# Pooled attention with a mixture-of-depths layer: one value load per batch, natural key order, no stores from GpSimd, a new order

## The chip, the core and the metric

The kernel runs on one core of a Trainium2 chip. The metric is the device time of one execution in microseconds (us). A profile is one execution recorded by the hardware: it gives the busy time of the engines (PE is the matmul engine, DVE the vector engine, ACT the scalar engine, POOL is GpSimd, SP the sync engine, which here only issues DMAs), the waits, and the traffic of the 16 DMA engines.

## The reference

Inputs are q, k and v of 8 batches, 8 heads, 576 tokens and 64 elements in float32, a gate vector and two weight matrices.

1. Keys and values are averaged over groups of 8 tokens, so each head has 72 pooled keys and values. Scores are q times pooled keys, scaled; softmax over the 72; output is the weighted sum of pooled values. The heads side by side make x of 576 x 512 per batch.
2. Each token of x gets a score by the gate vector. The 128 highest tokens of a batch (`capacity`) go through relu(x W1) W2, with W1 of 512 x 1024 and W2 of 1024 x 512; the result is multiplied by the sigmoid of the score and added to the token. All other tokens of x are returned as they are.

## The kernel before, in words

`direct_path` (line 253) does all of it; a general path behind a flag is not entered with these inputs. Step functions are named here by what they do, with the short names that the order tables use; `b` is the batch, `h` a half of the tokens, `c` one of five chunks of the tokens.

- **Loads.** `load_kq` (L472) and `load_v` (L485) issue them, all on SP's queue. Keys of a batch come in one load of 1.15 MB into the one buffer KR (`k`); queries in two of 0.64 and 0.51 MB (`q{b}{h}`); values of two heads side by side: 64 of the 72 pooled groups of each head on 128 partitions in four loads of 256 KB (`v{b}a` to `d`), the 8 groups left over of each head in four loads of 64 KB to 32 partitions each. Two of these four are copies of the other two, for two blocks of 32 partitions. In the main part group 9 of each nine is the leftover. Weights `w1{g}`, `w2{g}` are four loads of 1 MB.
- **Pooling.** Batch 0 is pooled on PE (`kP`, `vP`). Other batches on DVE or POOL (`kp`, `va`, `vb`), in place. `kh` transposes pooled keys in 32 x 32 blocks, `kt` (L546) adds the last pair and splits main keys from leftovers, `kl` (L551) spreads the leftover keys over a block of zeros. `vg`, `vt` give the values' part of the gate score, `vl` (L640) spreads the leftover values.
- **Attention.** `qt` transposes queries (DVE). `s` and `sl` are the scores of a half (PE, four PSUM banks that only one half can hold at a time), `x` and `xl` their exponentials (ACT), `a{b}{c}` weighted sums of a chunk (PE), `z`, `r`, `n` divide by the sum (ACT, DVE), `o{b}{c}` (L703) stores the chunk to the output in HBM: 256 KB, or 128 KB for chunk 4.
- **Selection.** `sc`, `sp`, `ke`, `c`, `oh`, `pk`, `tk` rank the tokens and find the 128 indices; `ix` (L768) on POOL gathers these rows from the output in HBM, for which all five stores of the batch must have landed.
- **Dense layers.** `tu` transposes the gathered rows, `u{b}{g}{f}` are the 8 column blocks of W1 (PE, L800; 8 matmuls each), `re` the relu, `d{b}{f}` the 8 row blocks of W2 (PE, L814), `y` the residual, `pt` (L822) on POOL scatters the rows to the output.

What sets the order: each step is registered with `add` in a `Plan` (L106); every engine runs its steps strictly in the order of the table ORDER (L48, a list of step numbers); HOMES picks the PSUM banks, and TURNS picks the engine where a step allows several (the costs that stand with the steps are used only when there is no table). A DMA of SP's or ACT's queue takes one of eight completion counters in turn, and the program makes it wait until the DMA eight places earlier in the table, of either queue, has landed. An engine that issues such a DMA waits there with all that is behind it. DMAs of POOL have counters of their own.

Of the kernel before, what the change touches and what calls it, by code (L numbers as in the profile page):

```python
# [11 lines left out]
OP = mybir.AluOpType  # L12
# [4 lines left out]
def kernel(  # L17
# [60 lines left out]
"""  # L78
HOMES = """
# [3 lines left out]
"""  # L83
TURNS = """
# [15 lines left out]
"""  # L100
TABLE = [[int(x) for x in t.split()] for t in (ORDER, HOMES, TURNS)]
ON_PE = (0,)
AGO = 500


class Plan:  # L106


    SWITCH = 0.2
# [143 lines left out]
def direct_path(ctx, tc, q, k, v, moe_w_gate, moe_w1, moe_w2, moe_capacity, out, flag):  # L253
# [6 lines left out]
    nc = tc.nc  # L260

    B, H, S, D = q.shape
    POOLW = 8
    SP = S // POOLW
    G = 16
# [150 lines left out]
    def opening():  # L416
# [12 lines left out]
        def line():  # L429
# [3 lines left out]
            for x in (*SS, *RZ):  # L433
                nc.gpsimd.memset(x, 0.0)
# [816 lines left out]
```

## Time and profile before

| what | value |
|---|---|
| runs shown | 263.66, 265.09, 265.61 us, median 265.09 us |
| profiled execution | 264.04 us, of which the span of instructions is 262.3 us |
| mean granted PE clock | 0.955 of full |
| busy in the span | PE 225.8 us (86%), DVE 150.5 us (57%), ACT 88.1 us (34%), POOL 99.9 us (38%) |
| DMA | 47.88 MB, of which HBM reads 35.78 MB |
| chain that ended last | DMA 38%, PE 37%, issue 7%, DVE 5%, POOL 5% of the span |

The time of the profiled execution has 1.74 us around the span. PE's busy share is not its efficiency: matmuls overlap, so the time that a stretch of work takes is read from the starts of the rows, not from their lengths. The 40 slices of the page show two stages: the DMA engines are at 0.97 or more of full use until about 80 us, and at 0.6 to 1.0 until 150 us; from 156 us on PE is busy nearly without a break until 252 us, and a tail of some 10 us follows (last residual, scatter and flag).

### The profile page before, as it was taken

How to read it: one execution, taken by the hardware profiler on the slowest of the kernel's cores; microseconds unless marked ns; L12 is line 12 of the kernel's file. 1: busy time of each engine (PE TensorE's matmuls, PEld its weight loads, DVE VectorE, ACT ScalarE, POOL GpSimd, SP SyncE). 2: the span in 40 equal slices, each digit the busy share in tenths (PEclk: the TensorE clock that was granted, in tenths of full speed). 3: DMA queues.
4: the chain of work that ended last, by engine and by line, in shares of the span. 5: the costliest groups of instructions: out<-in, count | busy, mean ns of one | idle time of the engine just before them, and what ended most of it. 6: DMA issues, size and time to landing. Idle time of an engine off the chain costs nothing.

```text
span 262.3 us, 7373 instructions
## 1 busy us (share of the span) xinstructions
PE 225.8 (86%) x3074; PEld 158.2 (60%) x3074; DVE 150.5 (57%) x346; ACT 88.1 (34%) x302; POOL 99.9 (38%) x154
## 2 busy tenths in 40 slices
PE   5599698974896899999898789999799989999960
PEld 5486546543485545974776356866399757759430
DVE  5059978654675567686887893848366136100310
ACT  1013566765124715811167232467141000110100
POOL 5014569925753266026073870112333520120120
PEclk9999979999799599999999979999999999999995
DMA  5999999999997768499968510013116520110120
GB/s 163 312 269 288 315 304 360 316 300 306 313 387 286 246 208 275 142 259 323 296 197 308 188 44 2 2 42 103 43 41 202 159 83 2 34 46 2 40 77 15
DMA packets 18413, 47.88 MB, mean 183 GB/s; under 512 B 2964, under 2 KB 2964, under 8 KB 17476
## 3 DMA queue, kind: packets, MB, share of 16 engines
q1 hardware_dynamic: 13776, 37.75, 45.1%
q0 software_dynamic: 2896, 6.76, 8.3%
q10 hardware_dynamic: 1700, 2.82, 3.3%
q8 instruction: 26, 0.43, 0.7%
q14 instruction: 15, 0.12, 0.1%
HBM read 35.78 MB, written 11.53 MB: 180 GB/s over the span
## 4 chain that ended last, share of the span: by engine, by line
DMA 38%; PE 37%; issue 7%; DVE 5%; POOL 5%; SPq 2%; ACT 2%; ACTq 0%; POOLq 0%; DVEq 0%
DMA qr<-in_q_dram 10%; PE pJ L800 9%; DMA vr<-in_v_dram 9%; DMA out_dram<-y,ix 6%; DMA w<-in_moe_w_dram 5%; PE pG L814 5%; PE pJ L814 4%; PE pG L800 4%; DMA out_dram<-xs 4%; DMA xr<-out_dram,ix 4%; PE pG L581 3%; PE pA L814 3%; SPq L400 2%; PE pA L658 2%; PE pG L590 2%
## 5 line engine op out<-in xcount | busy, mean ns | idle before, releaser
L800 PEld LDWEIGHTS pJ<-xg,w 128*128 128x128 f32 x352 | 41.6, 194 | 5.9 <-issue 5.1
L800 PE MATMUL pJ<-xg,w 128*128 128x128 f32 x352 | 43.6, 280 | 0.0
L744 DVE SCALAR_TENSOR_TENSOR cmp<-sr,sc,lat 128x576 bf16<-128x576 f32 (+1 forms) x40 | 36.6, 916 | 1.3 <-ACT sr L412 0.7
L814 PE MATMUL pJ<-w,ht 128*128 128x512 f32 x64 | 31.9, 636 | 0.0
L581 PE MATMUL pG<-qt,kt 32*64 32x256 f32 (+1 forms) x512 | 22.9, 447 | 3.5 <-issue 2.4
L563 DVE STREAM_TRANSPOSE qt<-qr 128x1280 f32<-128x1280 f32 (+1 forms) x16 | 21.8, 1365 | 5.9 <-DMA qr<-in_q_dram 5.8
L595 ACT ACTIVATE em<-pG 128x1280 f32<-128x1280 f32 (+1 forms) x16 | 18.2, 1138 | 11.7 <-PE pG L590 11.7
L623 POOL TENSOR_TENSOR vr<-vr 128x512 f32<-128x512 f32 (+1 forms) x11 | 16.7, 1541 | 7.4 <-DMA vr<-in_v_dram 3.8
L684 DVE RECIPROCAL rz<-za 128x8 f32<-128x8 f32 (+1 forms) x40 | 7.4, 190 | 20.9 <-ACT za L676 17.9
L814 PEld LDWEIGHTS pJ<-w,ht 128*128 128x128 f32 x64 | 11.9, 201 | 11.5 <-issue 11.1
L769 POOL TENSOR_SCALAR ix<-tk 128x1 int32<-128x1 f32 x8 | 2.3, 284 | 41.4 <-DVE gv L778 19.0
L581 PEld LDWEIGHTS pG<-qt,kt 32*64 32x64 f32 x512 | 10.5, 138 | 11.6 <-issue 7.7
L658 PEld LDWEIGHTS pG<-vs,em 64*64 64x64 f32 x528 | 13.0, 141 | 5.4 <-ACT em L595 3.0
L658 PE MATMUL pA<-vs,em 64*64 64x66 f32 x480 | 12.9, 224 | 3.8 <-issue 3.1
L814 PE MATMUL pA<-w,ht 128*128 128x512 f32 x32 | 15.8, 596 | 0.0
L823 POOL DMA_INDIRECT out_dram<-y,ix x8 | 8.7, 1088 | 18.4 <-DVE y L819 14.6
L658 PE MATMUL pG<-vs,em 64*64 64x66 f32 x528 | 13.9, 230 | 2.1 <-ACT em L595 2.1
L658 PEld LDWEIGHTS pA<-vs,em 64*64 64x64 f32 x480 | 10.8, 135 | 7.9 <-issue 5.4
L800 PEld LDWEIGHTS pG<-xg,w 128*128 128x128 f32 x128 | 14.8, 192 | 1.0 <-issue 1.0
L800 PE MATMUL pG<-xg,w 128*128 128x128 f32 x128 | 15.2, 276 | 0.0
L814 PE MATMUL pG<-w,ht 128*128 128x512 f32 x32 | 14.4, 592 | 0.0
L693 ACT ACTIVATE xs<-pA,rz 128x64 f32<-128x64 f32 (+1 forms) x64 | 14.0, 348 | 0.0
(173 smaller groups left out, 387.7 us busy)
## 6 DMA issues: line engine op xcount, KB each, us to landing
vr<-in_v_dram SPq DMA_DIRECT2D x32, 256.0 KB
kr<-in_k_dram SPq DMA_DIRECT2D x7, 1152.0 KB
qr<-in_q_dram SPq DMA_DIRECT2D x8, 640.0 KB
qr<-in_q_dram SPq DMA_DIRECT2D x8, 512.0 KB
w<-in_moe_w_dram SPq DMA_DIRECT2D x4, 1024.0 KB
out_dram<-xs SPq DMA_DIRECT2D x15, 256.0 KB
out_dram<-xs ACTq DMA_DIRECT2D x9, 256.0 KB
vr<-in_v_dram SPq DMA_DIRECT2D x32, 64.0 KB
```

The source lines that it names most:

```text
L400: i = engine(e).dma_start(out=dst, in_=src)
L563: nc.vector.transpose(out=QT[b % 2][h].rearrange("p j t c -> p t j c"), in_=QR[b % 2][h].rearrange("p t (j e) -> p t j e", j=2))
L581: note(nc.tensor.matmul(pG[64 * s : 64 * s + 64, r, 0:n], KT[i][rows, j, s, 0:NK], tokens(j, s, rows, 0, hi - lo), start=(j == 0), stop=(j ...
L595: note(nc.scalar.activation(EM[h][i], pG[:, :, 0:n], AF.Exp, scale=exp_scale))
L623: engine(e).tensor_tensor(out=x[:, a:z, 0:4], in0=x[:, a:z, 0:4], in1=x[:, a:z, 4:8], op=OP.add)
L658: note(nc.tensor.matmul(acc[64 * z : 64 * z + 64, s, E * m : E * m + E], EM[h][i][64 * s : 64 * s + 64, m, m0 + 64 * z : m0 + 64 * z + 64] ...
L684: nc.vector.reciprocal(RZ[i][rows, c], ZA[rows, b, c])
L693: note(nc.scalar.activation(to[:, s, m], o[:, s, m, 0:D], AF.Copy, scale=rz[:, NP * s + m : NP * s + m + 1]))
L744: nc.vector.scalar_tensor_tensor(cmp[0:n], SR[0:n], SC[i][0:n, c : c + 1], LAT[0:n, LAST - OFF[c] : LAST - OFF[c] + S], op0=OP.subtract, o ...
L800: note(nc.tensor.matmul(single(ju)[:, cap * f : cap * f + cap], w1[g][:, d, 128 * f : 128 * f + 128], XG[i][:, d, :], start=(d == 0), stop ...
L814: note(nc.tensor.matmul(single(jd)[0:cap, :], HT[i][f // 4][:, f % 4, :], w2[f // 4][:, f % 4, :], start=(f == 0), stop=(f == FB - 1)))
L823: j = nc.gpsimd.indirect_dma_start(out=out_rows, out_offset=bass.IndirectOffsetOnAxis(ap=IX[x][:, :1], axis=0), in_=Y[i], in_offset=None)
```

## The change

- Values: the main part of a batch is one load of 1 MB. Its partitions hold groups 8 to 71 of the even head and groups 0 to 63 of the odd head, which lie next to each other in HBM. The leftovers (groups 0 to 7 of the even, 64 to 71 of the odd head) come in two loads of 64 KB rather than four; the second copy of 32 partitions is made on the core, after pooling, by a new step `vd` of two small copies on ACT (5 batches) or DVE (3).
- Keys stay in natural order: `kt` adds all 288 pairs in one instruction, scores read shifted columns of it, `kl` is one instruction instead of two.
- Queries: one buffer and one load of 1.15 MB per batch (batch 0 keeps two).
- Stores `o` can no longer go to POOL. Before, 17 were on SP, 12 on ACT and 11 on POOL; after, 21 on SP and 19 on ACT.
- Four memsets on POOL at the start, 32 x 512 each.
- New ORDER, HOMES and TURNS. DMAs of SP and ACT: 123 before, 88 after.

```diff
-    QR = [[sb(f"qr{i}{h}", [128, hi - lo, D]) for h, (lo, hi) in enumerate(HALF)] for i in range(2)]
+    QR = sb("qr", [128, TG, D], n=2)
...
-        alts = (("SP", cost), ("ACT", cost), ("POOL", 0.75)) if free else (("SP", cost),)
+        alts = (("SP", cost), ("ACT", cost)) if free else (("SP", cost),)
...
+            for x in VR:
+                for z in (32, 96):
+                    nc.gpsimd.memset(x[z : z + 32, NP], 0.0)
...
+            dma(QR[b % 2], src, 128 * 256 * TG, p + 2, (), [("QR", b % 2, 0), ("QR", b % 2, 1)], name=f"q{b}")
...
-        for m in range(NP):
-            dma(VR[i][:, m], bass.AP(tensor=t, offset=o + 2 * m * head, ap=[[(NL + 1) * run, G], [run, NL], [1, run]]),
-                128 * 2048, p + 0.01 * m, [("VR", i, m // 2)], [("VRq", i, m)], name=f"v{b}{'abcd'[m]}", cost=0.6)
+        dma(VR[i][:, 0:NP], bass.AP(tensor=t, offset=o + NL * run, ap=[[run, 128], [2 * head, NP], [1, run]]),
+            128 * NP * 2048, p, [("VR", i, 0), ("VR", i, 1)], [("VRq", i, 0)], rate=390e3, name=f"v{b}", cost=0.6)
         for s in range(2):
-            src = bass.AP(tensor=t, offset=o + s * head + NL * run, ap=[[(NL + 1) * run, NL], [2 * head, NP], [1, run]])
-            for u in range(2):
...
+            dma(VR[i][64 * s : 64 * s + 32, NP], bass.AP(tensor=t, offset=o + s * (SP + NK) * run, ap=[[run, NL], [2 * head, NP], [1, run]]),
+                32 * 2048, p + 0.3 + 0.1 * s, [("VR", i, 1)], [("VRq", i, 1 + s)], rate=110e3, name=f"v{b}{s}", cost=0.65)
-    VQ = ((0, 1), range(2, 8))
+    VQ = ((0,), (0, 1, 2))
...
+            engine(e).tensor_tensor(out=KT[i][:, :, 0 : 2 * SP], in0=x[:, :, :, 0], in1=x[:, :, :, 1], op=OP.add)
...
+        def again(e):
+            for s in range(2):
+                of = VS[i][64 * s : 64 * s + 32, NP]
+                to = VS[i][64 * s + 32 : 64 * s + 64, NP]
...
+        both((("DVE", 0.35), ("ACT", 0.42)), False, again, [("VS", i)], [("VS2", i)], p, name=f"vd{b}")
```

The tables name steps by number. Decoded, these are the parts that the prediction speaks of (in the new table `v3` is the main load of batch 3, `v30` and `v31` its leftovers; in the old one a leftover has three digits):

```
SP before:  q01 v000 k01 k00 v1a v0b v0a v0c v0d v010 v001 v011 q00 v1b k1 v101 v100 v1d v111 v1c v110 q11 v2d k2
            v200 v2a v2c v201 v211 v210 v2b q10 q20 q21 v311 k3 o02 v3c v301 q40 v310 q31 q41 o04 v3a v300 q30 v3b
            w21 v3d w11 v4c w10 o13 v4b k4 w20 q51 o11 v410 v400 v411 v4a v4d v401 k5 ...
SP after:   k01 q01 k00 v0 v10 v01 v00 q00 k1 v11 v1 q1 k2 v2 q2 k3 v20 v21 v31 q3 v3 v30 w20 w10 o03 o04 k4 o11
            w11 o12 v41 o10 v4 o24 q4 v40 o23 w21 k5 v51 v50 v5 q5 ...
PE before:  ... pk0 sp10 a22 a20 a24 a21 tu0 sp11 s31 sl31 a23 u010 u011 s30 sl30 u012 u013 u000 u001 u002 u003
            sp21 a33 a32 a34 pk1 d00 ...
PE after:   ... pk0 sl31 a24 a20 s30 sl30 tu0 a32 a33 a30 u010 u011 u012 u013 u000 u001 u002 u003 pk1 a31 a34
            s41 sl41 d00 d01 d02 d03 tu1 s40 sl40 a44 ...
ACT after:  ... xl30 o14 ge0 xg0 o13 z30 z32 oh1 n32 re00 o21 z31 o32 z34 o31 o20 x41 xl41 n34 ...
POOL after: ... va30 va31 vb3 vg3 ix0 kp41 vl3 pc1 va40 va41 gp0 kt4 kl4 vb4 vg4 ix1 ...
Eight places before (new table): o14 after k4, o13 after v41, o32 after w21, o31 after v51, o20 after v50, o40 after k6
```

## Rows read from the trace of the kernel before

**Rows 1.** Stretches: us, busy of PE, PEld, DVE, ACT, POOL (instructions), PE clock, DMA share, GB/s.

```profile
60.00:70.00 10.00, 5.10 (x100) 3.00 (x100) 5.81 (x13) 3.44 (x19) 5.67 (x8) 0.90 1.04 312
80.00:90.00 10.00, 6.65 (x116) 4.70 (x114) 4.26 (x9) 6.19 (x20) 2.40 (x2) 0.75 0.64 237
156.00:252.00 96.00, 93.16 (x1004) 66.37 (x1003) 40.00 (x119) 22.68 (x65) 20.15 (x38) 1.00 0.19 57
```

**Rows 2.** The chain that ended last: start us, us, what.

```profile
56.93 14.20 DMA w<-in_moe_w_dram
...
102.22 1.05 PE pG L581 x32
103.27 0.57 PE pG L590 x16
103.84 0.63 PE pA L658 x32
104.47 0.45 PE pA L662 x8
...
245.38 6.88 PE pG L814 x16
```

**Rows 3.** PE's timeline at the first dense layer: start us, us, instructions, idle before and releaser.

```profile
66.80 0.63 PE L791 MATMUL pA<-ident,xr 128*128 128x128 f32 x4 [2.62 <-DVE qt L563]
72.26 2.05 PE L800 MATMUL pJ<-xg,w 128*128 128x128 f32 x16
86.35 1.16 PE L658 MATMUL pG<-vs,em 64*64 64x66 f32 x32 [1.88 <-ACT em L595]
```

**Rows 4.** ACT's timeline in the same stretch.

```profile
71.16 0.57 ACTq L400 DMA_DIRECT2D out_dram<-xs  x1
73.31 0.18 ACT L677 COPY ss<-pA 128x8 f32<-128x8 f32 x1
81.59 0.62 ACTq L400 DMA_DIRECT2D out_dram<-xs  x1
82.31 0.60 ACT L807 ACTIVATE ht<-pJ 128x512 f32<-128x512 f32 x1 [8.82 <-DVE qt L563]
85.29 1.00 ACT L595 ACTIVATE em<-pG 128x1024 f32<-128x1024 f32 x1
```

**Rows 5.** Stretches again, for the rate of the DMA engines (last column).

```profile
0.00:70.00 70.00, 53.20 (x951) 37.81 (x955) 45.57 (x93) 29.50 (x111) 36.12 (x62) 0.96 0.97 295
10.00:16.00 6.00, 6.00 (x22) 4.65 (x22) 1.48 (x9) 0.40 (x1) 0.00 (x0) 1.00 1.05 253
22.00:28.00 6.00, 5.41 (x141) 4.18 (x137) 5.64 (x10) 2.98 (x6) 1.51 (x1) 1.00 1.03 248
32.00:36.00 4.00, 3.10 (x56) 1.49 (x64) 3.22 (x8) 1.59 (x12) 3.16 (x3) 0.73 0.99 244
76.00:80.00 4.00, 4.00 (x37) 4.00 (x38) 3.93 (x9) 0.00 (x0) 0.00 (x0) 1.00 1.03 406
```

**Rows 6.** Groups by line and form: count, busy us, mean ns of one, idle before.

```profile
L400 POOL DMA_DIRECT2D out_dram<-xs x11 | 7.5, 684 | 6.9 <-DMA out_dram<-y,ix 5.3 <-ACT xs L693 1.5
L641 POOL TENSOR_TENSOR vl<-vs,inside 128x528 f32<-128x528 f32 x6 | 6.9, 1146 | 10.0 <-DVE rz L684 6.7 <-DVE vs L637 2.3 <-DMA kr<-in_k_dram 1.0
L532 POOL TENSOR_TENSOR kr<-kr 128x512 f32<-128x512 f32 x1 | 1.7, 1743 | 0.0
L533 POOL TENSOR_TENSOR ks<-kr 128x256 f32<-128x256 f32 x1 | 0.9, 861 | 0.1
L412 ACT COPY vs<-pG 128x128 f32<-128x128 f32 x1 | 0.3, 266 | 1.4 <-PE pG L613 1.4
L434 POOL MEMSET rz<- 128x40 f32 x2 | 0.2, 170 | 0.0
```

**Rows 7.** Who waited for whom: us in total, times, longest.

```profile
POOL kx L553 <- DVE kh L541: 24.2, 3, 13.1
```

**Rows 8.** Issues of chunk stores on ACT: ns min/median/max, first and last start.

```profile
L400 ACTq DMA_DIRECT2D out_dram<-xs x12: 564/614/1189, 39.1 to 202.9; - x12
```

More of the change, by code (lines that the diff above doesn't have):

```diff
@@ L305, in direct_path @@
     KH = sb("kh", [128, 2, 2 * G, R])
-    KT = sb("kt", [128, 2, 2, NK], n=2)
-    KX = sb("kx", [128, 2, 2, NL], n=2)
+    KT = sb("kt", [128, 2, 2 * (SP + NK)], n=2)
     KL = sb("kl", [128, 2, 2, NL, NP], n=2)
@@ L434, in line @@
                 nc.gpsimd.memset(x, 0.0)
+            for x in VR:
+                for z in (32, 96):
+                    nc.gpsimd.memset(x[z : z + 32, NP], 0.0)
             nc.gpsimd.memset(RK, -1.0)
-        add("POOL", 2.2, line, (), ["first", "slots"] + [(x, i, c) for x in ("SS", "RZ") for i in range(2) for c in range(NC)]
-            + [("RK", b, c) for b in range(B) for c in range(NC)], -89, name="line")
+        add("POOL", 3.4, line, (), ["first", "slots"] + [(x, i, c) for x in ("SS", "RZ") for i in range(2) for c in range(NC)]
+            + [("RK", b, c) for b in range(B) for c in range(NC)] + [("VR", i, 1) for i in range(2)], -89, name="line")
         def grid():
@@ L481, in load_kq @@
         src = q[b].rearrange("h (g t) d -> (h g) t d", g=G)
-        for h, (a, z) in enumerate(HALF):
-            dma(QR[b % 2][h], src[:, a:z], 128 * 256 * (z - a), p + 2 + 0.1 * h, (), [("QR", b % 2, h)], name=f"q{b}{h}")
+        if b == 0:
+            for h, (a, z) in enumerate(HALF):
+                dma(QR[0][:, a:z], src[:, a:z], 128 * 256 * (z - a), p + 2 + 0.1 * h, (), [("QR", 0, h)], rate=345e3, name=f"q{b}{h}")
+        else:
+            dma(QR[b % 2], src, 128 * 256 * TG, p + 2, (), [("QR", b % 2, 0), ("QR", b % 2, 1)], name=f"q{b}")
     def load_v(b):
@@ L487, in load_v @@
         o, t, run, head = v.offset + b * H * S * D, v.tensor, POOLW * D, S * D
-        for m in range(NP):
-            dma(VR[i][:, m], bass.AP(tensor=t, offset=o + 2 * m * head, ap=[[(NL + 1) * run, G], [run, NL], [1, run]]),
-                128 * 2048, p + 0.01 * m, [("VR", i, m // 2)], [("VRq", i, m)], name=f"v{b}{'abcd'[m]}", cost=0.6)
+        dma(VR[i][:, 0:NP], bass.AP(tensor=t, offset=o + NL * run, ap=[[run, 128], [2 * head, NP], [1, run]]),
+            128 * NP * 2048, p, [("VR", i, 0), ("VR", i, 1)], [("VRq", i, 0)], rate=390e3, name=f"v{b}", cost=0.6)
         for s in range(2):
-            src = bass.AP(tensor=t, offset=o + s * head + NL * run, ap=[[(NL + 1) * run, NL], [2 * head, NP], [1, run]])
-            for u in range(2):
-                x = 64 * s + 32 * u
-                dma(VR[i][x : x + 32, NP], src, 32 * 2048, p + 0.3 + 0.1 * s, [("VR", i, 1)], [("VRq", i, 4 + 2 * s + u)],
-                    rate=104e3, name=f"v{b}{s}{u}", cost=0.65)
-    VQ = ((0, 1), range(2, 8))
+            dma(VR[i][64 * s : 64 * s + 32, NP], bass.AP(tensor=t, offset=o + s * (SP + NK) * run, ap=[[run, NL], [2 * head, NP], [1, run]]),
+                32 * 2048, p + 0.3 + 0.1 * s, [("VR", i, 1)], [("VRq", i, 1 + s)], rate=110e3, name=f"v{b}{s}", cost=0.65)
+    VQ = ((0,), (0, 1, 2))
     def load_gate():
@@ L542, in k_trans @@
         add("DVE", 1.25, one, [("KS", 0), ("KS", 1)], ["KH"], 100 * b - 60, name=f"kh{b}")
-        x = KH.rearrange("p j c r -> p (j c r)").rearrange("p (a n two) -> p a n two", n=NL + 1, two=2)
+        x = KH.rearrange("p j c r -> p j (c r)").rearrange("p j (n two) -> p j n two", two=2)
         def two(e):
-            engine(e).tensor_tensor(out=KT[i].rearrange("p j s (a n) -> p (j s a) n", n=NL), in0=x[:, :, 0:NL, 0], in1=x[:, :, 0:NL, 1],
-                                    op=OP.add)
-        both((("DVE", 0.45), ("POOL", 0.63)), True, two, ["KH"], [("KT", i)], 100 * b - 60, name=f"kt{b}")
+            engine(e).tensor_tensor(out=KT[i][:, :, 0 : 2 * SP], in0=x[:, :, :, 0], in1=x[:, :, :, 1], op=OP.add)
+        both((("DVE", 0.45), ("POOL", 0.67)), True, two, ["KH"], [("KT", i)], 100 * b - 60, name=f"kt{b}")
         def three(e):
-            e = engine(e)
-            e.tensor_tensor(out=KX[i].rearrange("p j s a -> p (j s a)"), in0=x[:, :, NL, 0], in1=x[:, :, NL, 1], op=OP.add)
-            e.tensor_tensor(out=KL[i].rearrange("p j s n m -> p (j s) n m"),
-                            in0=KX[i].rearrange("p j s (n one) -> p (j s) n one", one=1).to_broadcast([128, 4, NL, NP]),
-                            in1=inrow.rearrange("p (a b m) -> p a b m", a=1, b=1).to_broadcast([128, 4, NL, NP]), op=OP.mult)
-        both((("DVE", 0.45), ("POOL", 0.6)), True, three, ["KH", "ident"], [("KL", i)], 100 * b - 60, name=f"kl{b}")
+            left = KT[i].rearrange("p j (s n one) -> p (j s) n one", s=2, one=1)[:, :, 0:NL]
+            engine(e).tensor_tensor(out=KL[i].rearrange("p j s n m -> p (j s) n m"), in0=left.to_broadcast([128, 4, NL, NP]),
+                                    in1=inrow.rearrange("p (a b m) -> p a b m", a=1, b=1).to_broadcast([128, 4, NL, NP]), op=OP.mult)
+        both((("DVE", 0.33), ("POOL", 0.42)), True, three, [("KT", i), "ident"], [("KL", i)], 100 * b - 60, name=f"kl{b}")
     def q_trans(b, h):
@@ L563, in go @@
             nc.vector.transpose(out=QT[b % 2][h].rearrange("p j t c -> p t j c"),
-                                in_=QR[b % 2][h].rearrange("p t (j e) -> p t j e", j=2))
+                                in_=QR[b % 2][:, lo:hi].rearrange("p t (j e) -> p t j e", j=2))
         add("DVE", 0.19 + 0.0653 * (hi - lo), go, [("QR", b % 2, h)], [("QT", b % 2, h)], 100 * b - 55 + 10 * h, name=f"qt{b}{h}")
@@ L580, in go @@
                     for s in range(2):
-                        note(nc.tensor.matmul(pG[64 * s : 64 * s + 64, r, 0:n], KT[i][rows, j, s, 0:NK],
+                        note(nc.tensor.matmul(pG[64 * s : 64 * s + 64, r, 0:n], KT[i][rows, j, (SP - NL) * s + NL : (SP - NL) * s + SP],
                                          tokens(j, s, rows, 0, hi - lo), start=(j == 0), stop=(j == 1)))
@@ L638, in pool_v @@
         add("DVE", 0.48, total, [("VS", i)], [("VR", i, 0), ("VR", i, 1), ("VS2", i)], p, name=f"vt{b}")
+        def again(e):
+            for s in range(2):
+                of = VS[i][64 * s : 64 * s + 32, NP]
+                to = VS[i][64 * s + 32 : 64 * s + 64, NP]
+                if e == "ACT":
+                    nc.scalar.copy(out=to, in_=of)
+                else:
+                    nc.vector.tensor_copy(to, of)
+        both((("DVE", 0.35), ("ACT", 0.42)), False, again, [("VS", i)], [("VS2", i)], p, name=f"vd{b}")
         def spread(e):
```

91 rows, old and new, of tables (HOMES, ORDER, TURNS) are left out of this document.

## The prediction, made before the changed kernel was run

> **What bounds the kernel now.** I read the stretches first. The time falls in two. From 156 us to the end of the matmuls at 252 us PE is busy for 93.2 of 96 us at the full clock and the DMA engines at a fifth [rows 1]; the chain ends there in PE's second dense layer [rows 2]. So the end is PE's, and a step counts only if it lets PE start its work sooner or takes a hole out of it. The holes lie before: in 60 to 70 us PE is busy for 5.1 of 10 us, in 80 to 90 us for 6.65, there at a mean clock of 0.75 [rows 1]. Then I read the chain for what ends these two.
>
> The first hole ends with weights. PE turns the gathered rows of batch 0 at 66.80 us, but the first column block of W1 starts at 72.26 us [rows 3], after the load `w11`, issued at 56.93 us, has landed 14.2 us later [rows 2]. 1 MB alone needs 2.6 us at 406 GB/s, so the load stood in a queue: the DMA engines are full from the start (0.97 over 70 us) but move 295 GB/s on average [rows 5]. The rate is lost where leftovers land: 253, 248 and 244 GB/s in three stretches in which three, four and four of these small loads come, against 406 GB/s in a stretch without [rows 5].
>
> The second hole is ACT's. Its store `o14` goes out at 71.16 us, just as `w11` lands, which stands eight places earlier in the table; it finished a copy at 73.5 us and then stood at the issue of the next store, `o12`, until 81.59 us; the relu and the exponential behind it came at 82.31 and 85.29 us, and PE's next chunk at 86.35 us [rows 3, 4]. The hole costs 3.35 us of idle time [rows 1] and, from 86.35 to 90 us at the half clock (1.2 of 2.4 GHz, the mean of 0.75 says so), some 1.8 us more: 5.2 us.
>
> **The parts.** The sum is made against the profiled execution, 264.0 us, which lies 1.05 us under the median of the runs.
>
> Leftover loads, 32 to 16. What one costs beyond its bytes: 10 to 16 us moved 1.52 MB, which at 406 GB/s takes 3.74 us, so 2.26 us are lost on three, 0.75 us each; the same in the other two stretches gives 0.58 and 0.40 us [rows 5]. I take their mean over eleven, 0.56 us; ends 0.40 and 0.75. Ahead of `w11` in SP's table stand 16 of them before and 8 after: 4.5 us less (3.2 to 6.0). But the new order puts more large loads and the stores ahead: summed by the table, 19.5 MB with `w11` before, 20.0 after. The rate without leftovers is 20.65 MB in 70 - 2 (before the first load) - 16 x 0.56 = 59 us, 0.35 MB/us [rows 5], so 0.5 MB is 1.4 us. `w11` lands at 71.16 - 4.5 + 1.4 = 68.1 us, and `k4`, 1.3 MB ahead of it, at 64.4 us.
>
> Four value loads of 256 KB in one of 1 MB. By the table the stretch with 406 GB/s holds loads of 256 KB to 1.15 MB and shows no size that is slow, so by bytes and rate this is worth nothing; 64 issues on SP become 24, and SP is no bound. The Trainium skill ("DMA: Bandwidth & Descriptors", Rules for kernel authors) asks for at least 1 MiB per DMA for the full rate and calls transfers under 64 KB mostly overhead. If loads of 256 KB paid what leftovers do, the twelve fewer in four batches, at 0.56 us, would take 6.7 us more off the way to `w11`; no run here shows such a price, and the sum is made without it.
>
> The new order at the first dense layer. PE no longer waits for `w11` alone: `s30`, `a30`, `a32` and `a33` now come before `u010`, all of batch 3. Prices: a half's scores 1.05 + 0.57 = 1.62 us, a chunk 0.63 + 0.45 = 1.08 us [rows 2], so 4.9 us of work moves into the hole of 60 to 70 us. But these chunks need `vl3`, and on POOL that is now behind `kp41`, which needs `k4`: 64.4 + 1.74 + 0.86 for `kp41`, + 1.15 for `vl3` [rows 6], + 3.24 for three chunks gives 71.4 us, with 0.2 us for the hand-overs 71.6 us for `u010`, against 72.26. So the dense stage starts 0.7 us sooner and with 4.9 us less left to do: -5.6 us (ends 0, where the batch-3 work is late by as much as it is worth, and -8.9 us, where `w11` alone decides).
>
> Later leftovers, eight less, 4.5 us of DMA time after 72 us. There the DMA engines are no longer full (0.64 in 80 to 90 us [rows 1]), so most of it is beside PE's work: I take -1.5 us, ends 0 and -4.5.
>
> Stores off POOL. Eleven issues of 0.68 us and 6.9 us of waiting leave POOL [rows 6]; four go to SP and seven to ACT at 0.61 us [rows 8], 4.3 us more on an engine that is busy for a third. Beside other work they cost nothing; if ACT is late for PE at each, 4.3 us. With `vd` I take +0.5 us. `vd` is two small copies per batch, nearest a copy of 128 x 128 at 0.27 us [rows 6], so 0.5 us per batch between `vt` and `vl`; POOL and PE have other steps in between, and without these all eight would cost 4.3 us.
>
> Queries in one load: the half that is scored first waits for all 1.15 MB, 1.9 us longer at 0.35 MB/us for its 0.64 MB partner. Where the old order loaded the halves apart the second came much later, so I take 0, ends -2 and +2. The memsets on POOL (nearest 0.17 us [rows 6]; for 512 columns at most a few times that) lie in a wait of 13.1 us [rows 7]; one `kt` of 288 pairs and one instruction less in `kl`: nothing. Both are covered unless POOL becomes late; then about 1 us once.
>
> Sum: -5.6 - 1.5 + 0.5 = -6.6 us: 257.4 us for a profiled execution, 258.5 us as a median. The ends of the terms, not all at once, span 251 to 266.
>
> **Rivals.** *More than that:* the second hole closes too, because `w20` and `w10` now land before `w11`, so that fewer large loads are still under way when ACT comes to its stores. Against it: the new table still has ACT issuing four stores there. It gives 5.2 us more, 253, and with the full wire gain down to 247. Chance 0.16.
>
> *Nothing gained:* the bound of the first stage is not the wire but the chain pooling, transposes, ranking on DVE and POOL (DVE busy 45.6 of 70 us [rows 5], with waits for loads among the rest); then `u010` comes as much later as it has more done before it, and the time is 262.5 to 267. For it: `vl3` behind `kp41` as above. Chance 0.18.
>
> *Slower:* ACT stands behind stores. Seven more are on ACT, and each waits for the DMA eight places earlier, which is now `k4` for `o14`, `v41` for `o13`, `w21` for `o32`, leftovers of batch 5 for `o31` and `o20`, `k6` for `o40`: loads of 1 MB or small ones queued behind such. The price of one such stand that reaches PE is 5.2 us, as above. The profile already has one of 8 us [rows 4]. It decides from two more stands on that reach PE: 258.5 + 2 x 5.2 = 269 us. For it: `x41`, which `a44` needs, stands behind four stores in ACT's table. Against it: PE has the whole first layer of batch 0 and four `d` in front of `a44`. Chance 0.18.
>
> That the change does not do what it says (a leftover's price is one of the batch, not of the load, so that two cost what four did) leaves 1 MB less to read, 3 us over the run; it is in the second rival.
>
> **The numbers.** My forecast, 253 to 262, has 0.48. About 1% is what a measurement of this kernel can tell from no change, so the bounds are 262.4 and 267.7 us. Faster: 0.48 + 0.16 = 0.64; same 0.18; slower 0.18. The range leaves 0.05 below and 0.13 above: 248 to 267.
>
> **What would show it.** Right: `w11` lands near 68 us, the rate over the first 70 us is 310 GB/s or more, `u010` starts at 71 to 72 us with four steps of batch 3 behind it, and 156 to the end is full as before, some 6 us earlier. Wrong: a first 70 us no faster on the wire (then a leftover's price is elsewhere); ACT idle for over 5 us in front of an issue of a store and PE idle behind it (the slower rival); PE waiting for `vl3` or for a transposed query with the loads long landed (nothing gained).

## The result and the profile after

The changed kernel takes 252.67 us in the median (249.60 to 256.79), beside 264.53 us for the kernel before; the ratio is 0.9475 with a 95% interval of 0.9377 to 0.9574. Two later comparisons give 0.9504 (0.9340 to 0.9669) and 0.9507 (0.9400 to 0.9614). So it is faster by 5%, some 13 us, where 6.6 us were forecast. Runs of one kernel spread by some 3%, and the ratios here and below are made from those within 1.5% of each kernel's fastest.

| profiled execution | before | after |
|---|---|---|
| time, span | 264.04, 262.3 us | 249.60, 247.8 us |
| busy PE, DVE, ACT, POOL | 225.8, 150.5, 88.1, 99.9 us | 220.0, 146.1, 83.4, 106.9 us |
| DMA | 47.88 MB | 46.82 MB |
| last load issued | 143.81 us | 112.35 us |
| chain: PE, DMA | 37%, 38% | 60%, 16% |

The stretches of the kernel after that answer to [rows 1, 5], with the end of the run at 240 where it was at 252 (columns as there):

```profile
0.00:70.00 70.00, 53.14 (x1043) 36.94 (x1043) 54.27 (x103) 31.59 (x111) 39.03 (x63) 0.95 0.91 322
10.00:16.00 6.00, 5.23 (x33) 4.33 (x32) 4.48 (x14) 0.27 (x1) 0.99 (x1) 1.00 1.01 350
32.00:36.00 4.00, 2.69 (x79) 1.50 (x80) 2.81 (x6) 2.74 (x10) 3.16 (x4) 1.00 0.96 339
60.00:70.00 10.00, 8.03 (x181) 5.42 (x174) 8.52 (x19) 6.86 (x19) 5.70 (x6) 1.00 0.81 288
80.00:90.00 10.00, 10.00 (x157) 7.76 (x157) 6.68 (x16) 4.18 (x16) 4.89 (x6) 1.00 0.83 309
156.00:240.00 84.00, 83.63 (x671) 57.93 (x664) 29.96 (x98) 14.32 (x45) 15.68 (x23) 1.00 0.18 60
```

The wire moves 322 GB/s over the first 70 us, not 295, and the stretch 80 to 90 us has no hole and the full clock. Now PE at the first dense layer, the timeline of after that answers to [rows 3]:

```profile
70.97 1.09 PE L796 MATMUL pA<-ident,xr 128*128 128x128 f32 x4 [2.94 <-DMA xr<-out_dram,ix]
...
77.15 7.41 PE L805 MATMUL pA<-xg,w 128*128 128x128 f32 x64
```

The first dense block starts at 77.15 us, 4.89 us later than before, with the 4.9 us of batch 3 ahead of it done. So at this point nothing is gained (in two more profiles of the changed kernel the block starts at 75.48 and 75.63 us): the whole difference of 14.5 us between the two spans arises behind it. Adding up PE's timelines from there to the last matmul: before 181.0 us (72.26 to 253.26) with 10.7 us of idle time in seven holes over 0.4 us; after 163.5 us (77.15 to 240.68) with 2.8 us, 2.2 of them in two such holes. Idle time is 7.9 us less; in the two more profiles it is 5.6 and 3.9 us rather than 2.8, so that this part is 5 to 8 us. Of the rest, 170.3 and 160.7 us, 4.9 us are the moved work and 4.7 us are work done faster, for which the clock is the row to read. In 75 to 100 and in 130 to 160 us, the kernel before:

```profile
75.00:100.00 25.00, 21.65 (x291) 14.06 (x276) 16.05 (x37) 9.46 (x33) 9.05 (x9) 0.86 0.74 264
...
130.00:160.00 30.00, 26.63 (x404) 17.38 (x397) 24.52 (x42) 13.85 (x55) 18.70 (x22) 0.94 0.53 173
```

and after:

```profile
75.00:100.00 25.00, 24.00 (x313) 16.36 (x306) 13.08 (x31) 10.11 (x37) 16.06 (x20) 0.96 0.86 323
...
130.00:160.00 30.00, 29.70 (x542) 24.87 (x549) 23.10 (x68) 15.89 (x53) 7.90 (x11) 1.00 0.25 75
```

A clock of 0.86 over 25 us and 0.94 over 30 us takes 5.3 us of full-speed work away, 0.96 and 1.00 take 1.0: 4.3 of the 4.7 us. The half clock stood behind PE's holes; with the holes went the half clock. The last 1.9 us are the tail, 9.0 us from the last matmul to the end before and 7.1 after: before, the last scatter is issued 3.5 us behind the one ahead of it (250.02 and 253.49 us) and its packets end 3.8 us later; after, it is issued 7.0 us behind (233.77 and 240.73) and they end 2.6 us later. That the scatter ahead holds the last one up is not shown. The tail goes with the order: 9.4 and 9.0 us in two profiles of the new loads in the old order, 6.8 and 7.9 with the old loads in the new. 7.9 + 4.7 + 1.9 = 14.5 us.

### The profile page after: what moved, and what is told of

Read it like the earlier page. It is cut to its first block, busy times and chain, and to the rows that moved or that the text cites. A ratio compares the mean times of both kernels' runs of the same rounds, so it can differ in the third digit from the quotient of the medians.

```text
span 247.8 us, 7329 instructions
## 1 busy us (share of the span) xinstructions
PE 220.0 (89%) x3074; PEld 155.9 (63%) x3074; DVE 146.1 (59%) x357; ACT 83.4 (34%) x282; POOL 106.9 (43%) x147
## 2 busy tenths in 40 slices
DMA packets 16329, 46.82 MB, mean 189 GB/s; under 512 B 1696, under 2 KB 1696, under 8 KB 14496
## 4 chain that ended last, share of the span: by engine, by line
PE 60%; DMA 16%; POOL 11%; issue 5%; DVE 4%; SPq 1%; POOLq 0%; DVEq 0%; ACT 0%
PE pJ L819 10%; PE pG L805 9%; DMA xr<-out_dram,ix 8%; DMA vr<-in_v_dram 8%; PE pA L805 7%; PE pJ L805 7%; PE pG L819 6%; PE pG L663 3%; PE pA L819 3%; POOL vr L618 3%; PE pG L667 2%; PE pG L576 2%; POOL vr L623 2%; POOL vs L624 1%; POOL vr L628 1%
## 5 line engine op out<-in xcount | busy, mean ns | idle before, releaser
L819 PE MATMUL pJ<-w,ht 128*128 128x512 f32 x80 | 37.7, 602 | 0.0
L805 PEld LDWEIGHTS pG<-xg,w 128*128 128x128 f32 x192 | 22.4, 192 | 1.8 <-issue 1.8
L805 PE MATMUL pG<-xg,w 128*128 128x128 f32 x192 | 23.1, 276 | 0.0
L819 PEld LDWEIGHTS pJ<-w,ht 128*128 128x128 f32 x80 | 14.0, 190 | 14.0 <-issue 13.6
L576 PE MATMUL pG<-qt,kt 32*64 32x320 f32 (+1 forms) x512 | 20.8, 429 | 1.3 <-ACT em L590 1.3
L805 PEld LDWEIGHTS pJ<-xg,w 128*128 128x128 f32 x160 | 18.6, 192 | 1.8 <-issue 1.4
L805 PEld LDWEIGHTS pA<-xg,w 128*128 128x128 f32 x160 | 18.5, 192 | 1.8 <-issue 1.8
L805 PE MATMUL pJ<-xg,w 128*128 128x128 f32 x160 | 19.4, 277 | 0.0
L805 PE MATMUL pA<-xg,w 128*128 128x128 f32 x160 | 19.0, 276 | 0.0
L698 ACT ACTIVATE xs<-pG,rz 128x64 f32<-128x64 f32 (+1 forms) x56 | 12.1, 348 | 4.0 <-DMA out_dram<-xs 3.4
```

The lines of the kernel that those rows point to most:

```text
L576: note(nc.tensor.matmul(pG[64 * s : 64 * s + 64, r, 0:n], KT[i][rows, j, (SP - NL) * s + NL : (SP - NL) * s + SP], tokens(j, s, rows, 0, h ...
L698: note(nc.scalar.activation(to[:, s, m], o[:, s, m, 0:D], AF.Copy, scale=rz[:, NP * s + m : NP * s + m + 1]))
L805: note(nc.tensor.matmul(single(ju)[:, cap * f : cap * f + cap], w1[g][:, d, 128 * f : 128 * f + 128], XG[i][:, d, :], start=(d == 0), stop ...
L819: note(nc.tensor.matmul(single(jd)[0:cap, :], HT[i][f // 4][:, f % 4, :], w2[f // 4][:, f % 4, :], start=(f == 0), stop=(f == FB - 1)))
```

## The experiments

The change has three parts that can be set one by one: the loads with the steps that belong to them, the order (with banks and engines), and the 11 stores that POOL issued. Each ratio is to the kernel before on the same chip; the comparisons ran on several chips, so kernels of different comparisons are set side by side by their ratios.

### Loads, order and stores, one by one

Loads alone (new loads and steps; order, banks and engines of before; 11 stores on POOL), twice, and order with stores alone:

```diff
 new loads:  ORDER, HOMES, TURNS of before, v{b} where the second of its four loads stood
-        alts = (("SP", cost), ("ACT", cost)) if free else (("SP", cost),)
+        alts = (("SP", cost), ("ACT", cost), ("POOL", 0.75)) if free else (("SP", cost),)
 old loads:  ORDER, HOMES, TURNS of after, each load cut in 2 or 4 in its place
```

> The changed kernel's steps (loads, natural key order, copies of the leftovers) under the order, PSUM banks and engines of the kernel before; a merged load stands where the second of its parts stood, 11 stores stay on POOL. Theory W (the gain comes from less DMA time: the loads end 30 us sooner and PE finds its later work ready): 0.95 to 0.97 of before, about 252 to 257 us. Theory O (the order makes the gain: PE starts the dense layers with more work stored up): 0.985 to 1.00, 260 to 264.5 us.

> The new steps and loads alone (old order, stores on GpSimd), again with more rounds, since the first comparison gave it a median (257.1 us against 263.8) and no interval. If the loads alone carry what the prediction summed up (6.6 us), 256 to 259 us, ratio 0.967 to 0.98; if they carry more, and the order and the stores less, 251 to 255 us, ratio 0.95 to 0.965.

> The loads and key order of the kernel before (four value loads, four leftover loads, two query loads per batch) under the new order, PSUM banks and engines, all stores on SP and ACT. Theory W: no gain or slower, 0.985 to 1.02, 260 to 270 us, because SP's queue is as slow as before. Theory O: most of the gain stays, 0.95 to 0.97.

The changed kernel with its 11 stores back on POOL, and the kernel before with only these moved off it (7 to SP, 4 to ACT, as in the changed kernel), the latter with the old and with the new loads:

```diff
 TURNS, o03 o10 o00 o22 o20 o24 o34 o23 o53 o64 o63
-0 or 1 (SP or ACT)
+2 (POOL), and the other way round
```

> The changed kernel with eleven stores on POOL again (the chunks that were there before), at the places that the new order gives them. If taking the stores off POOL is part of the gain: 2 to 5 us slower than the changed kernel, 0.955 to 0.97 of before. If it is worth nothing, or ACT is better off without them: 0.94 to 0.955.

> The kernel before with its order and its loads, and only the 11 stores that GpSimd issues given to SyncE (7) and ScalarE (4), the queues that they have in the changed kernel. The prediction priced this part at +0.5 us (ends below nothing to +4.3), since GpSimd's 7.5 us in the stores seemed covered. Putting the stores back on GpSimd in the changed kernel cost 3.4 per cent. Theory A (a store on GpSimd costs its engine where GpSimd is the one that is late, whatever the order): 257 to 261 us, ratio 0.975 to 0.99. Theory B (it costs only in the new order, where GpSimd has the gathers and the pooling of the second half earlier, and the old order was made round those stores): 262 to 266 us, ratio 0.995 to 1.01. If SyncE or ScalarE stands behind the stores and late loads follow, over 267 us, ratio above 1.01.

> The changed kernel's steps and loads under the order and engines of the kernel before, and the 11 GpSimd stores given to the queues that they have in the changed kernel: loads and stores changed, order not. With the stores on GpSimd this kernel took 257.1 us, ratio about 0.975; with the old loads, moving the 11 stores cost 4.6 per cent. Theory A (a store that moves off GpSimd stands behind loads and waits in a queue whose order was not made for it; the cost belongs to the old order): 264 to 270 us, ratio 1.0 to 1.025. Theory B (the stores stood behind the small loads; with 2 in place of 4 leftover loads and fewer loads in the queues the wait is gone): 254 to 259 us, ratio 0.965 to 0.98, and then the new order is worth only the 2 to 3 per cent between this and the changed kernel.

> The last of the eight combinations: the old loads under the new order, with the 11 stores on GpSimd. The other seven gave: old order, old loads 1 (on GpSimd) and 1.046 (off); old order, new loads 0.975 and 0.964; new order, old loads 1.013 (off); new order, new loads 0.981 (on) and 0.948 (off). Theory A (stores off GpSimd only pay where the loads no longer hold up the queues; with the old loads they cost): with the stores back on GpSimd this kernel is faster than 1.013, 255 to 262 us, ratio 0.97 to 0.995. Theory B (the new order needs GpSimd free, whatever the loads): slower than 1.013 by as much as with the new loads, 270 to 276 us, ratio 1.02 to 1.045.

Measured, all eight combinations:

| loads | order | 11 stores | median us | ratio (95%) |
|---|---|---|---|---|
| old | old | POOL | 263.8 to 265.8 | 1 |
| old | old | SP, ACT | 274.65 | 1.046 (1.034 to 1.059) |
| old | new | POOL | 264.62 | 1.013 (0.999 to 1.026) |
| old | new | SP, ACT | 264.32 | 1.013 (0.999 to 1.026) |
| new | old | POOL | 251.33 (first time 257.1) | 0.961 (0.952 to 0.970) |
| new | old | SP, ACT | 254.49 | 0.964 (0.959 to 0.969) |
| new | new | POOL | 257.68 | 0.981 (0.964 to 0.998) |
| new | new | SP, ACT | 252.67, 250.89, 248.09 | 0.948, 0.950, 0.951 |

The loads are worth 3.2 to 8.2 points in each of the four pairs; alone they give 3.9 (2.5 the first time, without an interval), some 10 of the 13 us. The order and the stores give nothing or cost by themselves. Together they add about 1 point to the loads (248.09 beside 251.33 us in one comparison; the intervals of the two ratios overlap). The stores off POOL cost 4.6 points in the old kernel, nothing with the new loads or the new order alone (intervals that lie on each other), and are worth 3 points in the changed kernel. Of the expectations, the loads alone came out at theory W, and when repeated at the second outcome, the old loads under the new order at theory W. The stores back on POOL in the changed kernel cost more than either outcome allowed. The old loads without POOL stores came out at the third, slow outcome, the new loads without them at theory B, and the last cell at neither: the price of a store's queue is not its own.

Why it turns sign is seen at the store of batch 0's first tile, `o00`, which goes to ACT. The old loads without POOL stores, timelines of ACT, POOL and PE:

```profile
52.85 0.16 ACT L677 COPY ss<-pJ 128x8 f32<-128x8 f32 x1
58.52 0.61 ACTq L400 DMA_DIRECT2D out_dram<-xs  x1
59.18 1.58 ACT L751 ACTIVATE apart<-slots,rk 128x128 f32<-128x128 f32 x5 [6.17 <-DMA out_dram<-xs]
...
68.31 1.10 POOL L770 DMA_INDIRECT xr<-out_dram,ix  x1 [5.37 <-PE pA L662]
...
76.97 1.08 PE L791 MATMUL pA<-ident,xr 128*128 128x128 f32 x4 [7.88 <-DMA xr<-out_dram,ix]
```

The new loads, same order, same queues:

```profile
47.38 0.61 ACTq L396 DMA_DIRECT2D out_dram<-xs  x1
48.03 1.57 ACT L756 ACTIVATE apart<-slots,rk 128x128 f32<-128x128 f32 x5 [0.40 <-POOL ks L531]
...
56.89 1.10 POOL L775 DMA_INDIRECT xr<-out_dram,ix  x1 [2.14 <-issue]
...
63.39 1.09 PE L796 MATMUL pA<-ident,xr 128*128 128x128 f32 x4 [5.49 <-DMA xr<-out_dram,ix]
```

With the old loads ACT stands 6.17 us at the issue, and the masks of the ranking, the gather and PE's first turn of gathered rows follow 11 to 14 us later than with the new loads; some 5 us of these are there before the stand, since the copy at 52.85 us comes at 47.48 with the new loads. By the tables the DMA eight places ahead of `o00` is `v310` with the old loads, a leftover of batch 3 in a full queue, and `k3` with the new, long landed. That store alone put back on POOL, under the old loads:

```diff
 TURNS, o00
-1 (ACT)
+2 (POOL)
```

> The kernel before (its order, its loads) with 10 of the 11 GpSimd stores given to SyncE and ScalarE, and one, the store of batch 0's first tile, left on GpSimd. The kernel with all 11 moved took 274.65 us (ratio 1.046): in its trace ScalarE stands 6.17 us behind that one store (issued at 58.52 us), the ranking's masks come after it, and the gather xr is issued at 68.31 and lets TensorE wait 7.88 us to 76.97. Theory A (ScalarE behind the store is the cost): with that store back on GpSimd the masks start at about 53 to 55 us, the first dense block starts 5 us or more earlier, 265 to 269 us, ratio 1.0 to 1.025. Theory B (the stores that SyncE issues stand behind loads there, so the gather that reads the stored rows is late whatever ScalarE does): the gather's issue moves by less than 2 us, 271 to 276 us, ratio 1.035 to 1.05.

272.55 us, 1.030 (1.023 to 1.037), between the theories: 1.6 points of the 4.6, with intervals that just overlap. ACT's and PE's timelines of that kernel show why no more:

```profile
92.65 0.61 ACTq L400 DMA_DIRECT2D out_dram<-xs  x1
93.31 1.57 ACT L751 ACTIVATE apart<-slots,rk 128x128 f32<-128x128 f32 x5 [8.38 <-DMA out_dram<-xs]
95.65 1.00 ACT L595 ACTIVATE em<-pG 128x1024 f32<-128x1024 f32 x1
...
69.06 1.09 PE L791 MATMUL pA<-ident,xr 128*128 128x128 f32 x4 [8.00 <-DMA xr<-out_dram,ix]
96.70 1.16 PE L658 MATMUL pG<-vs,em 64*64 64x66 f32 x32 [10.38 <-ACT em L595]
```

The first turn comes 7.9 us sooner, and then ACT stands 8.38 us at a later store of the ten, with PE idle for 10.38 us behind it. In the changed kernel ACT's stores of that stretch go out at 84.61, 85.88, 87.33 and 87.98 us with no such stand, where before one stood 8 us [rows 4].

With the stores on POOL in the changed kernel, the loss is mostly at the second gather: PE takes its rows at 97.28 us, and at 93.41 without them. By the second batch's first dense block, behind a granted clock of 0.50 from 95.2 to 102.0 us, the 3.9 us have become 6.0 (110.67 and 104.67) of the 7.1 us between the two spans (timeline of PE, stores on POOL):

```profile
97.28 1.11 PE L796 MATMUL pJ<-ident,xr 128*128 128x128 f32 x4 [4.79 <-DMA xr<-out_dram,ix]
```

### Which of the loads

Leftovers in four loads (no `vd`, no memsets), main values in four of 256 KB, queries in two, each in the place of its one step in the changed kernel, and combinations:

```diff
 leftovers
+                for u in range(2):
+                    x = 64 * s + 32 * u
+                    nc.sync.dma_start(out=VR[i][x : x + 32, NP], in_=src)
 main values
+            for m in range(NP):
+                nc.sync.dma_start(out=VR[i][:, m], in_=bass.AP(tensor=t, offset=o + NL * run + 2 * m * head, ap=[[run, 128], [1, run]]))
 queries
+                for h in ((0, 1) if b in (1,) else (1, 0)):
+                    a, z = HALF[h]
+                    nc.sync.dma_start(out=QR[b % 2][:, a:z], in_=src[:, a:z])
```

> The changed kernel with four leftover loads of 64 KB per batch again (both blocks of 32 partitions loaded) and without the copies on the core and the memsets; all else, the order too, as changed. If a leftover load costs 0.56 us of DMA time beyond its bytes and the DMA engines set the time of the first stage: 5 to 9 us slower than the changed kernel, 257 to 261 us (0.97 to 0.985 of before). If the leftovers do not matter: as the changed kernel, 0.945 to 0.955.

> The changed kernel with the main values of a batch in four loads of 256 KB instead of one of 1 MB. The prediction priced this part at 0 us. Theory (the size of these loads is worth little; what counts is the number of small leftover loads and the order): 251 to 254.5 us, within 1 per cent of the changed kernel in the same comparison, the 16 DMA engines' busy time within 2 us of 132.8. Rival (large loads are better used by the DMA engines, and much of the 18 us of their time that the change saved is from these): 256 to 259 us, 1.5 to 2.5 per cent more than the changed kernel, the DMA engines' busy time 6 to 12 us above 132.8, and inputs later from the second batch on.

> The changed kernel with the queries of each batch after the first in two loads, as before, at the place of the one. The prediction priced this part at 0 us (ends 2 either way). Theory (size and number of these loads are worth nothing in this order, since a batch's first half is not needed before its second has landed): 250 to 254 us, within 1 per cent of the changed kernel. Rival (7 issues of 0.4 us more on SyncE and another place in the round of waits for earlier transfers delay what is behind them): 255 to 258 us, ratio 0.96 to 0.975.

> The changed kernel with main values in four loads and queries in two, leftover keys in two as changed. Each alone is within 1 per cent of the changed kernel. Theory A (they add up to nothing): 248 to 252 us, ratio 0.945 to 0.957. Theory B (the number of loads a batch counts together): 253 to 258 us, ratio 0.965 to 0.98.

> The changed kernel with every load cut as before at the place of its one step: main values in four of 256 KB, four leftover loads a batch, queries in two; the key order, the order of the steps and the stores stay as changed. Alone, four leftover loads cost 2.5 per cent (0.9725 against 0.9475), the four main loads nothing resolved (0.9537 against 0.9504) and the two query loads nothing (0.9469). Theory A (the parts add up: only the leftover loads count): 254 to 257 us, ratio 0.97 to 0.98, and the rest of the distance to 1.013 of the old loads under this order comes from the key order's steps. Theory B (the number of loads counts only together, since each further one is issued later behind earlier transfers): 260 to 266 us, ratio 0.99 to 1.015.

| of the changed kernel made small | median us | ratio (95%) |
|---|---|---|
| nothing | 252.67, 250.89, 248.09 | 0.948, 0.950, 0.951 |
| main values | 251.91 | 0.954 (0.919 to 0.989) |
| queries | 250.06 | 0.947 (0.942 to 0.952) |
| main values and queries | 248.01 | 0.941 (0.934 to 0.948) |
| leftovers | 254.55 | 0.973 (0.962 to 0.983) |
| all | 255.62 | 0.970 (0.964 to 0.977) |
| all, with the old key order and its steps | 264.32 | 1.013 (0.999 to 1.026) |

The size of the main and query loads is worth nothing that these runs resolve, alone or together; the interval of the main values alone is wide, the row with both is the firmer one. The Trainium skill ("DMA: Bandwidth & Descriptors", Rules for kernel authors) wants at least 1 MiB per DMA for the most bandwidth; here the loads of 256 KB give 0.941 to 0.954 and the loads of 1 MB 0.948 to 0.951, so the measurement decides for no difference. Four leftovers in place of two, without `vd` and the memsets, cost about 2.3 points, 6 us. So main values, queries and both together came out at the theory that they are worth nothing, leftovers and all small at the theory that the leftovers count. The last step, 4.3 points or 11 us between two comparisons, has the same loads by size and number and differs in the key order: from which addresses the values are read, how `kt` and `kl` are made, and which load waits for which part of the value buffer. The profiles show one part of this in the loads themselves, since packets and bytes are the same. Old key order, new order of steps (SP's queue: packets, MB, share of 16 engines over a span of 260.0 us):

```profile
q1 hardware_dynamic: 14048, 38.28, 43.8%
```

All small in natural key order (span 252.3 us):

```profile
q1 hardware_dynamic: 14048, 38.28, 42.6%
```

That is 113.9 and 107.5 us of the DMA engines' time, 2.98 and 2.81 us per MB. The same quotient splits all kernels by their key order: 2.98 to 3.18 us per MB in the five with the old (the kernel before 3.13), 2.70 to 2.82 in all with the new, whatever the number and size of their loads (2.81 with four leftovers, 2.77 in the changed kernel). The packet records of the two traces say where the difference lies. The 9472 packets of 2 KB (values, weights and SP's stores, of which only the values were read from other addresses) took 61.0 us in the old key order and 55.3 in the natural one, all other packets of SP's queue 52.9 and 52.3. Of the 9472, 2240 took 100 to 150 ns each in the old order and 263 in the natural one; the leftovers have only 1024 packets, so it is not they alone. How much of the 11 us is this and how much the steps was not separated.

### What is left in the first stage

The changed kernel's hole before the ranking, timelines of SP, DVE, ACT and PE:

```profile
32.53 0.33 SPq L396 DMA_DIRECT2D kr<-in_k_dram  x1
...
40.87 0.69 DVE L530 TENSOR_TENSOR kr<-kr 128x512 f32<-128x512 f32 x1 [2.96 <-DMA kr<-in_k_dram]
...
44.91 1.74 ACT L698 ACTIVATE xs<-pJ,rz 128x64 f32<-128x64 f32 x8 [3.46 <-DVE rz L689]
...
46.71 1.16 PE L663 MATMUL pJ<-vs,em 64*64 64x66 f32 x32 [3.68 <-ACT xs L698]
```

`k3` waits for the one key buffer, DVE for `k3`, ACT for DVE, PE for ACT. Hence two key buffers; then three steps more on other engines, in two versions:

```diff
-    KR = sb("kr", [128, TG, D])
+    KR = sb("kr", [128, TG, D], n=2)
 then TURNS: vd2 from DVE to ACT; o31 and o20 from ACT to POOL (first version) or to SP (second)
```

> The changed kernel with two buffers for a batch's keys instead of one, nothing else. Its trace shows the load of k3 issued at 32.53 us, when GpSimd ended the last addition in the one key buffer (31.77 + 0.73), and landed for VectorE at 40.87, with VectorE idle 2.96 us and TensorE idle 3.69 us (43.02 to 46.71) and then at half clock to 52.5 behind it. Theory (the first stage is now set by when inputs come, the key buffer among them): k3 issues at 23 to 25 us, the hole at 43 closes, the first dense block starts 4 to 7 us before 77.15, and the kernel takes 246 to 250 us, ratio 0.925 to 0.94. Rival (VectorE and GpSimd set the first stage by their own work; another load is late in its place): the wait goes to v3 or q3 and then to the ranking, the first dense block still starts at 75 to 78 us, 251 to 254 us, ratio 0.945 to 0.955.

> The changed kernel with two key buffers (248.8 us measured for that alone) and three steps on other engines, the order kept: the copies of batch 2's leftover value sums from VectorE (2.88 us at 47.46, at half speed beside GpSimd) to ScalarE, and two stores that ScalarE waits behind at 84.47 (5.43 us, with TensorE idle 2.20 us behind it at 89.26) to GpSimd, which is idle from 82.91 to 86.05. Theory (these are the waits that end last there): the holes at 50.9, 53.2 and 89.3 close, first dense block 2 to 3 us earlier, 243 to 247 us, ratio 0.92 to 0.935. Rival (the next thing is late in their place, the gather or the leftover loads): 247 to 250 us, ratio 0.935 to 0.95.

> The changed kernel with two key buffers, the copies of batch 2's leftover value sums on ScalarE, and the two stores behind which ScalarE stood at 84.47 us given to SyncE, which has nothing to issue between 84.9 and 92.8. With those two on GpSimd its queue stood behind them instead and the second gather was 6.95 us late (ratio 0.955). Theory (with the stores in a queue that is idle then, neither ScalarE nor the gather is late): the holes near 86 to 92 shrink by 2 to 4 us against the kernel with two key buffers alone, 244 to 248 us, ratio 0.925 to 0.94. Rival (the second gather, which reads the stored rows, is late whichever queue stores them, so the gain of the first stage is taken back there): 248 to 251 us, within 1 per cent of the changed kernel.

Two buffers alone: 248.79 us beside 250.89 for the changed kernel, 0.951 beside 0.950, not resolved (the theory by its time, the rival by its ratio), though the hole at 43 us is 0.63 us and the first dense block starts at 71.49. With the two stores on POOL the second gather is late, as its PE timeline shows, and nothing is gained: 254.59 us, 0.955 (0.948 to 0.962), slower than both outcomes:

```profile
92.79 1.12 PE L796 MATMUL pJ<-ident,xr 128*128 128x128 f32 x4 [6.95 <-DMA xr<-out_dram,ix]
```

With them on SP: 245.45 us, 0.938 (0.928 to 0.949), beside 248.09 for the changed kernel on the same chip; the six runs (243.13 to 246.63) all lie under its six (246.78 to 249.96). This version is faster than the kernel before, and by 1% than the changed kernel, as its theory had it. That the gain comes from where it was expected is not shown: in its profile the first dense block starts at 74.71, between the others, after a gather that PE waits for 3.39 us; what is smaller is the idle time behind it, 2.0 us.

## Why the forecast was half of the gain

The time falls inside the range of 248 to 267 us, but not by the working: the sum's main term came to nothing, and what made the gain had been put at 1.5 us.

**First dense block at 71.6 us, -5.6 us: wrong.** It came at 77.15 us with the same work ahead of it, so the term was 0, its upper end (-1.6 and -1.5 by the two more profiles), as in the rival "nothing gained". `w11` was not in the way any more, nor `vl3`, which POOL had ended at 69.84 us: PE waited for the gathered rows `xr`, and POOL issued that gather only when the ranking was done. POOL's timeline of after:

```profile
63.88 0.81 POOL L774 TENSOR_SCALAR ix<-tk 128x1 int32<-128x1 f32 x1 [6.22 <-DVE gv L783]
64.99 1.20 POOL L775 DMA_INDIRECT xr<-out_dram,ix  x1 [0.30 <-POOL ix L774]
```

The step took `tu0` as free and asked only for weights and values. The wire did get better as said (322 GB/s against at least 310), but the first stage was then bound by the key buffer and the ranking behind it. With two key buffers the block starts where it was forecast, at 71.49 us. PE's timeline of that kernel:

```profile
68.03 0.63 PE L796 MATMUL pA<-ident,xr 128*128 128x128 f32 x4 [0.50 <-DVE cmp L749]
68.59 0.70 PE L663 MATMUL pJ<-vs,em 64*64 64x66 f32 x32
...
71.49 3.73 PE L805 MATMUL pA<-xg,w 128*128 128x128 f32 x31
```

and of the changed kernel, one row between the two shown above:

```profile
71.99 1.16 PE L663 MATMUL pJ<-vs,em 64*64 64x66 f32 x32
```

So the 5.7 us between the two starts are 2.9 us by which the rows came later and 2.7 us by which the four steps of PE behind them took longer (6.2 rather than 3.5 us), at a granted clock of 0.50 from 70 to 76.5 us. The forecast had a price for neither. With the new loads in the old order the block starts at 70.24 us, 2.0 us sooner than before.

**Later leftovers, -1.5 us (ends 0 and -4.5): far too small.** The step held that past 72 us the DMA engines are not full, so that saved transfers lie beside PE's work. But they were late for PE all the same: with the new loads alone, in the old order, the time from the first dense block to the last matmul is 175.2 us (70.24 to 245.40) where it was 181.0, so 5.8 us for all that the loads changed. Of the 10.7 us of holes behind the first dense block four, 5.1 us, stand behind ACT at its stores (81 and 84 us), a transposed query (124) and a chunk's division (142); three, 5.5 us, behind gathers. PE's timeline of before, where [rows 3] has the second of the seven:

```profile
82.96 0.43 PE L732 MATMUL pJ<-ident,sc 128*128 128x128 f32 x2 [1.47 <-ACT ht L807]
...
125.47 1.12 PE L581 MATMUL pG<-qt,kt 32*64 32x256 f32 x32 [1.09 <-DVE qt L563]
...
142.54 0.69 PE L658 MATMUL pA<-vs,em 64*64 64x66 f32 x16 [0.68 <-DVE xs L695]
...
152.05 0.65 PE L791 MATMUL pJ<-ident,xr 128*128 128x128 f32 x4 [2.69 <-DMA xr<-out_dram,ix]
...
187.44 0.63 PE L791 MATMUL pJ<-ident,xr 128*128 128x128 f32 x4 [1.89 <-DMA xr<-out_dram,ix]
...
216.04 0.66 PE L791 MATMUL pG<-ident,xr 128*128 128x128 f32 x4 [0.95 <-DMA xr<-out_dram,ix]
```

The new loads alone, in the old order (a run of 256.54 us):

```profile
142.84 0.66 PE L796 MATMUL pJ<-ident,xr 128*128 128x128 f32 x4 [1.45 <-DMA xr<-out_dram,ix]
...
177.55 0.63 PE L796 MATMUL pJ<-ident,xr 128*128 128x128 f32 x4 [2.09 <-DMA xr<-out_dram,ix]
...
208.18 0.66 PE L796 MATMUL pG<-ident,xr 128*128 128x128 f32 x4 [0.88 <-DMA xr<-out_dram,ix]
```

There the four are gone and the gathers' holes are 4.4 us. So the loads took the first kind and their share of half clock. In the changed kernel the gathers' holes are 2.2 us, but 4.2 and 3.9 in its two more profiles, so that order and stores took a share of the second kind is not shown. The rival "more than that" had the size (253 us) and one of the holes, 80 to 90 us, right.

**0.56 us for a leftover beyond its bytes: mis-sized, for a wrong reason.** 16 leftovers more, in natural key order, cost 137.8 - 132.8 = 5.0 us of the DMA engines' time, 0.31 us each (0.23 to 0.41 against the three profiles of the changed kernel); at 2.77 us per MB 64 KB are 0.18, which leaves 0.13 us (0.05 to 0.23), not 0.56, and less than the forecast's lower end of 0.40. The slow stretches of [rows 5] held main loads in the old key order too, and their slowness, 3.13 against 2.77 us per MB over the run, was put on the leftovers. The packet records of before bear this out: in the three stretches 447 of 588, 194 of 375 and 273 of 399 packets of 2 KB took 100 to 150 ns, more than the 96 and twice 128 that leftovers have there, and in the stretch at 406 GB/s none of 253. The natural key order was priced by its instructions alone, at nothing; it was the part with no row, and its addresses were not bounded at all. That leftovers are worth some 6 us in time, near the 7.1 of the first two terms, is no proof of the price.

**Stores off POOL, +0.5 us: wrong for the changed kernel, and with the wrong sign.** -3 points (8 us) there, +4.6 points (12 us) in the old one; nothing that is resolved with the new loads alone or the new order alone, so near the forecast in the two combinations that it was not made for. The stand of ACT behind stores, the slower rival's mechanism, is real: 6.17 and 8.38 us above. In the changed kernel ACT's stores of that stretch had no such stand; that the new loads had landed by then is shown for `o00` under the old order and argued for the rest.

**1 MB loads, the query load, 0 each: right**, by experiments. **`vd`, covered: right but for one place.** Ten copies on ACT take 245 ns each, near the 0.27 us taken; one pair on DVE took 2.86 us beside POOL's pooling, where the other two pairs took 0.38 us, so some seven times as long and not the half speed that an expectation above read there. **156 us to the end full: right.** The tail's 1.9 us were not seen.

## What to carry to other kernels

A transfer stage that no longer fills the wire can still be what makes the compute stage ragged: look at when the last load is issued, not only at the stretch where the DMA engines are full, and count the half clock behind each hole with the hole. The price of an issue moved to another queue is the wait for what stands ahead there, so it changes sign with the other parts of a change; price it in the order and with the loads that it will have. A changed address pattern is a term of its own even where bytes, packets and instructions stay.

## What the runs showed of the hardware

Two kernels whose SP queue moved the same 14048 packets and 38.28 MB differed in its transfer time: 2.98 us per MB with value loads from 16 separate runs of 8 groups of 2 KB, 2.81 with one run of 128. The difference lies in the packets of 2 KB, of which 2240 and 263 took 100 to 150 ns. Two small copies of 32 x 66 took 2.86 us on DVE beside POOL's additions, 0.38 us on DVE at other times, and 0.50 us on ACT in the same kernel.
